# Gated attention and two mixtures on one Trainium2 core: the attention's products ordered by the shape of their tiles, and the chunk ends of two head pairs limited and inverted together

## The chip, the cores and the metric

The kernel runs on one core of a Trainium2 chip. Five engines work side by side, each through its own queue and in its own order: TensorE (PE; its weight loads are listed apart as PEld), VectorE (DVE), ScalarE (ACT), GpSimd (POOL) and SyncE (SP), which here issues most of the transfers. Semaphores hold an instruction back until what it needs is there. The metric is the device time of one execution in microseconds (us); lower is better.

## What is computed

```python
f = 1/(1+exp(-f_logit))                       # B,H,S,D = 4,8,768,48
for t in range(S):
    state = f[:,:,t,:,None]*state + einsum('bhd,bhe->bhde', k[:,:,t], v[:,:,t])
    y[:,:,t] = einsum('bhd,bhde->bhe', q[:,:,t], state)
x = y.transpose(0,2,1,3).reshape(B*S, H*D)    # 3072 tokens of 384
logits = x @ w_gate                           # 8 experts, 384 tokens each,
# given out greedily by descending logit; a token has one expert e
out[mask] = relu(x[mask] @ w1[e]) @ w2[e]     # 384 -> 1024 -> 384
h = out @ w_in;  result = (h*clip(h+3,0,6)/6) @ w_out      # 384 -> 2048 -> 384
```

All arrays are float32.

## The kernel before

The first fifth of the time is the attention (function `attention`); the routing of the tokens and the eight experts follow, and nothing of them is changed.

The attention goes over chunks of 128 time steps (C=128): 4 batches of 768 steps are 24 chunks (NCH), three of them a unit (U=384, NU=8). Two heads of 48 rows, padded to 64, share the 128 partitions, so that eight heads are four pairs (NP=4, index p). Within a chunk the recurrence is turned into products: `P` is the running product of the gates from the start of a chunk, `S` that from the other end divided by the whole product at the chunk's end, `QT` is q times P, `KH` is k times S, and the state is carried from chunk to chunk.

For each unit and pair, `tgroup` (L70 to L106) transposes f, k or q by three TensorE products (L83) into one of three PSUM buffers `pT`, and hands back a list of VectorE work: for f, after ScalarE has written the gate to `ff` (L87), the scan P (L91), the limit of its three chunk ends (L92), their reciprocal into the start values `m1` (L93) and the scan S (L94); for k the product KH (L96); for q the product QT (L103). `group` (L108) puts this work on VectorE's queue one or two calls later, and `ORD` (L198) gives the order of the twelve (pair, name) of a unit. A loop over j (L227) takes one chunk per step, and in it four groups of the next unit:

- `a_mm` (L134): the scores of chunk j+1, eight products from 64 rows to 128 columns, in two halves;
- `l_mm` (L189): the output of chunk j-1 for the store and the router's logits, four products of 128 by 128;
- `tg(0)`, `tg(1)`, `tg(2)`, `tg(3)`: the transposes, 128 by 128;
- `a_ev`: ScalarE copies the scores to SBUF (L139), GpSimd masks them (L140);
- `y_mm`: the output of chunk j, for each pair two products of the state (L161, 64 rows to 64 columns) and two of the masked scores (L163, 128 rows to 64 columns), summed in PSUM tile `pY`, which ScalarE copies (L165);
- `kv_mm` (L175): the chunk's part of the new state, 128 rows to 64 columns, added by VectorE (L182) and scaled by GpSimd (L183);
- `kt_mm` (L147): KH of chunk j+1 transposed, 128 by 128, copied by ScalarE (L148). Tile `pM` serves `kt_mm` and `l_mm` in turn.

Every sixth step starts a batch and has no state product; the step before it has no `kv_mm`, and the one before that no `kt_mm`. In the trace a product of float32 appears as two instructions on TensorE, a transpose as one. `prep` spreads the splitting of the last layer's weights over these steps: four VectorE operations per 128x512 tile (L876, L878, L880, L883), two of ScalarE and one of GpSimd (L664). `refill` reorders the next unit's f (ScalarE), k and q (GpSimd) and starts the loads after it.

Of the kernel before, what the change touches and what calls it, by code (L numbers as in the profile page):

```python
# [13 lines left out]
B,H,S,D=4,8,768,48  # L14
C=128; U=384; NP=4; NU=B*S//U; NCH=B*S//C
PMIN=2.0**-60; PB=3; MB=1

def attention(tc, q,k,v,f,wg, x_dram, lg, ident, pmin, ranges, prep, setup, spin):
    nc=tc.nc
    ctx=ExitStack()  # L20
    with ctx:
# [13 lines left out]
        M1=[]  # L35
        for i in range(2):
            t=cs.tile([128,U],F32,name=f"m1{i}"); nc.vector.memset(t,0.0); M1.append(t)
# [31 lines left out]
        KH={};QT={};PC={};tmp={}  # L69
        def tgroup(u,p,nm):  # L70
            if p==0 and nm=='f':
                t=wk.tile([128,NP,3],F32,name="pc",bufs=3); PC[u]=t
            if p==0 and nm=='k':
                KH[u]=KHB[u%2]
            if p==0 and nm=='q':
                t=wk.tile([128,NP,U],F32,name="qt"); QT[u]=t
            if u==0:
                n=ORD.index((p,nm))%4
                pt=ps.tile([128,C*3],F32,name=("pT","pA0","pT","pA1")[n],bufs=PB if n%2==0 else 1).rearrange("p (c r) -> p c r",r=3)
            else: pt=ps.tile([128,C,3],F32,name="pT",bufs=PB)  # L80
            x=perm[nm]
            for r in range(3):
                nc.tensor.transpose(pt[:,:,r],x[:,r,p].rearrange("p a d -> p (a d)"),ident)  # L83
            pf=pt.rearrange("p c r -> p (c r)")
            if nm=='f':
                ff=FF[p%2]
                nc.scalar.activation(ff[:,:U],pf,AF.Identity,bias=half[:,0:1],scale=0.5)  # L87
                P=wk.tile([128,U],F32,name="P",bufs=3); S_=wk.tile([128,U],F32,name="S")
                tmp[u,p]=(P,S_)
                V=nc.vector; m1=M1[p%2]; ends=lambda t: t.rearrange("p (c t) -> p c t",t=C)[:,:,C-1]  # L90
                return ([lambda: V.tensor_tensor_scan(P,m0,ff[:,:U],1.0,op0=OP.max,op1=OP.mult),  # L91
                         lambda: V.tensor_scalar(PC[u][:,p],ends(P),PMIN,None,op0=OP.max)],  # L92
                        [lambda: V.reciprocal(ends(m1),PC[u][:,p]),  # L93
                         lambda: V.tensor_tensor_scan(S_[:,::-1],ff[:,1:U+1][:,::-1],m1[:,::-1],1.0,op0=OP.mult,op1=OP.max)])  # L94
            elif nm=='k':
                return [lambda: nc.vector.tensor_mul(KH[u][:,p],pf,tmp[u,p][1])],[]  # L96
            else:
                if u==0:
                    t=wk.tile([128,2,NP,C],F32,name="am").rearrange("p s a c -> p (s a c)")[:,:U]
                    nc.scalar.copy(t,pf)  # L100
                    nc.gpsimd.tensor_tensor(out=QT[u][:,p],in0=t,in1=tmp[u,p][0],op=OP.mult)
                def whole_q():
                    if u>0: nc.vector.tensor_mul(QT[u][:,p],pf,tmp[u,p][0])  # L103
                    if p==NP-1:
                        nc.vector.tensor_tensor(out=pmin,in0=pmin,in1=PC[u].rearrange("p a b -> p (a b)"),op=OP.min)
                return [whole_q],[]  # L106
        prev=([],[]); rest=[]; late=[]
        def group(new,fill=None,flush=False):  # L108

# [12 lines left out]
                for op in prev[0]: op()  # L122
                prev=([],prev[1])
        AM={};KT={};pA={}
        def a_mm(j,hf):
            u,c=divmod(j,3)
            if hf==0:
                pA[j]=[]
                for s in range(2):
                    t=ps.tile([128,NP,C],F32,name=f"pA{s}"); pA[j].append(t)  # L130
            for p in (0,1) if hf==0 else (2,3):
# [9 lines left out]
        def kt_mm(j):  # L141
# [8 lines left out]
        YT={}  # L150
        def y_mm(j):
            u,c=divmod(j,3); first=j%6==0
            vr=raw['v',u]; cc=slice(c*C,(c+1)*C)
            last=j==NCH-1
            yt=wk.tile([128,NP,C],F32,name="yt")
            if not last: py=ps.tile([128,NP,C],F32,name="pY")
            for p in range(NP):
                if last and p%2==0: py=ps.tile([128,NP,C],F32,name=f"pA{p//2}")
                rows=[slice(64*s,64*s+64) for s in range(2)]
                if not first:  # L160
                    for r in rows: nc.tensor.matmul(py[r,p],St[j%2][r,p],QT[u][r,p,cc],start=True,stop=False)  # L161
                for s,r in enumerate(rows):
                    nc.tensor.matmul(py[r,p],vr[:,c,2*p+s],AM[j][:,s,p],start=first,stop=True)  # L163
# [148 lines left out]
class Routing:  # L312
# [714 lines left out]
```

## Time and profile before

| | us |
|---|---|
| median of 3 runs | 912.87 (912.25 to 913.35) |
| the profiled execution, its own time | 914.29 |
| its span in the profile | 912.3 |
| TensorE busy | 865.5 (95%) |
| VectorE busy | 542.2 (59%) |
| ScalarE, GpSimd busy | 370.5, 300.8 |
| attention's loop, from the first scores to the last logits | 17.78 to 199.74 |

A matmul's busy time overlaps that of its neighbours, so the distance between starts tells more than the busy share. "issue" is idle time for which the profile shows no awaited event.

### The profile page before, as it was taken

To read this page: it belongs to the slowest core of one execution; us is meant where nothing else is said; L and a number is where in the kernel's file an instruction comes from. 1 tells how busy PE (TensorE), PEld (TensorE's weight loads), DVE (VectorE), ACT (ScalarE), POOL (GpSimd) and SP (SyncE) were. 2 spreads that over 40 slices of the span, in tenths; PEclk is the share of its full clock that TensorE was granted. 3 is DMA by queue.
4 is the path that set the end of the run, shared out by engine and by line. 5 is a ranking of instruction groups with operands and counts; after the bars stand their busy time and mean duration, and the time that the engine had idled before them with its cause. 6 is when DMAs were issued, how large, how long until landed. Compare 5 with 4: busy or idle time off the path is not lost.

```text
span 912.3 us, 16113 instructions
## 1 busy us (share of the span) xinstructions
PE 865.5 (95%) x6086; PEld 787.8 (86%) x6086; DVE 542.2 (59%) x1410; ACT 370.5 (41%) x741; POOL 300.8 (33%) x378
## 2 busy tenths in 40 slices
PE   7999999997897869999999999999999999999995
PEld 6767777776787769989999999999999999999995
DVE  7889888735867893584476465565575422431331
ACT  4555555422344351443144235415432642542331
POOL 7666654313311551242042214312340341331001
PEclk9999999995898999999999999999999999999998
DMA  9674694125122430221121112121220221110000
GB/s 248 184 190 98 176 256 102 35 70 166 36 70 75 143 95 18 78 79 35 35 79 53 61 38 68 42 73 44 61 87 4 75 83 32 53 52 27 1 1 31
DMA packets 77159, 71.92 MB, mean 79 GB/s; under 512 B 29200, under 2 KB 65040, under 8 KB 77072
## 3 DMA queue, kind: packets, MB, share of 16 engines
q1 hardware_dynamic: 74000, 61.37, 23.7%
q0 software_dynamic: 3072, 9.44, 3.2%
q8 instruction: 49, 0.80, 0.4%
q14 instruction: 38, 0.31, 0.1%
HBM read 61.35 MB, written 9.44 MB: 78 GB/s over the span
## 4 chain that ended last, share of the span: by engine, by line
PE 56%; issue 14%; DVE 9%; ACT 3%; POOL 2%; DMA 1%; SPq 0%; POOLq 0%; ACTq 0%; DVEq 0%
PE pF L667 8%; PE acc L667 8%; PE pF L668 8%; PE pF L669 8%; PE acc L669 7%; PE acc L668 7%; DVE ga L800 2%; PE pY L163 1%; PE pY L161 1%; PE pM L189 1%; POOL wol L664 1%; ACT ga L799 1%; PE pA L134 1%; PE pT L83 1%; DVE q_Lm L418 1%
## 5 line engine op out<-in xcount | busy, mean ns | idle before, releaser
L667 PE MATMUL pF<-xh,wih 128*128 128x384 f32 x384 | 134.1, 349 | 0.6 <-ACT xh L784 0.6
L667 PE MATMUL acc<-woh,hh 128*128 128x384 f32 x384 | 133.8, 348 | 0.0
L800 DVE SCALAR_TENSOR_TENSOR ga<-ga,pF 128x384 f32<-128x384 f32 x128 | 70.8, 553 | 101.8 <-ACT ga L799 101.5
L669 PE MATMUL acc<-wol,hh 128*128 128x384 f32 x384 | 131.2, 342 | 0.0
L668 PE MATMUL acc<-woh,hl 128*128 128x384 f32 x384 | 131.0, 341 | 0.0
L669 PE MATMUL pF<-xl,wih 128*128 128x384 f32 x384 | 130.5, 340 | 0.0
L668 PE MATMUL pF<-xh,wil 128*128 128x384 f32 x384 | 130.4, 340 | 0.0
L664 POOL TENSOR_TENSOR w1l<-wst,w1h 128x512 fp32r<-128x512 f32 x42 | 55.1, 1312 | 193.0 <-ACT w1h L663 193.0
L799 ACT ACTIVATE ga<-pF,three 128x384 f32<-128x384 f32 x128 | 74.1, 579 | 97.0 <-PE pF L669 96.9
L802 ACT CAST hh<-ga 128x384 fp32r<-128x384 f32 x128 | 65.7, 513 | 105.2 <-DVE ga L800 105.2
L803 DVE TENSOR_TENSOR hl<-ga,hh 128x384 fp32r<-128x384 f32 x128 | 71.4, 558 | 59.9 <-ACT hh L802 59.5
L664 POOL TENSOR_TENSOR w2l<-wst,w2h 128x384 fp32r<-128x384 f32 x58 | 60.1, 1040 | 112.2 <-ACT w2h L663 108.3
L765 ACT ACTIVATE hh<-pF 128x384 fp32r<-128x384 f32 x64 | 31.5, 492 | 127.0 <-PE pF L669 121.1
L766 DVE SCALAR_TENSOR_TENSOR hl<-pF,hh 128x384 fp32r<-128x384 f32 x64 | 35.6, 556 | 77.8 <-ACT hh L765 77.3
L667 PEld LDWEIGHTS pF<-xh,wih 128*128 128x128 f32 x384 | 73.0, 190 | 1.9 <-ACT xh L784 0.9
L669 PEld LDWEIGHTS acc<-wol,hh 128*128 128x128 f32 x384 | 73.5, 191 | 0.0
L668 PEld LDWEIGHTS acc<-woh,hl 128*128 128x128 f32 x384 | 73.5, 191 | 0.0
L667 PEld LDWEIGHTS acc<-woh,hh 128*128 128x128 f32 x384 | 73.4, 191 | 0.1
L669 PEld LDWEIGHTS pF<-xl,wih 128*128 128x128 f32 x384 | 72.9, 190 | 0.3 <-DVE xl L785 0.3
L668 PEld LDWEIGHTS pF<-xh,wil 128*128 128x128 f32 x384 | 73.0, 190 | 0.0
L667 PE MATMUL pF<-xh,w1h 128*128 128x384 f32 x192 | 67.3, 350 | 0.6 <-ACT xh L735 0.6
L669 PE MATMUL acc<-hl,w2h 128*128 128x384 f32 x192 | 65.1, 339 | 2.2 <-DVE hl L766 2.2
(289 smaller groups left out, 1799.0 us busy)
## 6 DMA issues: line engine op xcount, KB each, us to landing
wst<-in_moe_w_dram SPq DMA_DIRECT2D x58, 192.0 KB, 2.4
wst<-in_moe_w_dram SPq DMA_DIRECT2D x42, 256.0 KB, 2.7
pw<-in_moe_w_in_dram SPq DMA_DIRECT2D x12, 512.0 KB, 4.0
pw<-in_moe_w_out_dram SPq DMA_DIRECT2D x16, 384.0 KB, 3.1
v<-in_v_dram SPq DMA_DIRECT2D x24, 192.0 KB, 5.1
x_dram<-y SPq DMA_DIRECT2D x24, 192.0 KB, 3.8
fr<-in_f_logit_dram SPq DMA_DIRECT2D x7, 576.0 KB, 5.4
kr<-in_k_dram SPq DMA_DIRECT2D x7, 576.0 KB, 5.1
```

Of the source, the lines that this page charges most:

```text
L83: nc.tensor.transpose(pt[:,:,r],x[:,r,p].rearrange("p a d -> p (a d)"),ident)
L134: nc.tensor.matmul(pA[j][s][:,p],KH[u][r,p,c*C:(c+1)*C],QT[u][r,p,c*C:(c+1)*C],start=True,stop=True)
L664: eng_lo.tensor_tensor(out=lo, in0=raw, in1=hi.bitcast(F32), op=OP.subtract)
L667: nc.tensor.matmul(out, ahi, bhi, start=start, stop=False)
L668: nc.tensor.matmul(out, alo, bhi, start=False, stop=False)
L669: nc.tensor.matmul(out, ahi, blo, start=False, stop=stop)
L765: nc.scalar.activation(hh,p,AF.Relu)
L766: s.defer(2,lambda: nc.vector.scalar_tensor_tensor(hl,p,0.0,hh.bitcast(F32),op0=OP.max,op1=OP.subtract))
L799: nc.scalar.activation(a,p,AF.Relu,bias=s.three[:,0:1])
L800: late(f,1,lambda: nc.vector.scalar_tensor_tensor(g,a,6.0,p,op0=OP.min,op1=OP.mult))
L802: late(f,1,lambda: nc.scalar.copy(gh,g))
L803: late(f,3,lambda: nc.vector.tensor_tensor(out=gl,in0=g,in1=gh.bitcast(F32),op=OP.subtract))
```

## The change

1. **Order of the products.** The two halves of `a_mm` become one. `tg(0)`, `l_mm` and `tg(1)` now come first; then `y_mm` part 0 does all state products of chunk j, then `a_mm` of chunk j+1, then `y_mm` part 1 all score products of chunk j, then `kv_mm`, `tg(2)`, `kt_mm`, `tg(3)`. One PSUM tile holds the sums of all four pairs between the two parts of `y_mm`.
2. **Chunk ends in pairs.** P of two pairs stands in one tile; the limit and the reciprocal are one operation each on six values per partition, after the second scan. `ORD` brings the two f of such a pair one after the other, and the second S is done one call after the first.
3. The places of `prep`'s pieces are moved (`PREP`: two, one and three calls in the three steps of a unit, where it was two in each), and `refill` of f, q and k follows the new order.

```diff
-                P=wk.tile([128,U],F32,name="P",bufs=3); S_=wk.tile([128,U],F32,name="S")
...
-                return ([lambda: V.tensor_tensor_scan(P,m0,ff[:,:U],1.0,op0=OP.max,op1=OP.mult),
-                         lambda: V.tensor_scalar(PC[u][:,p],ends(P),PMIN,None,op0=OP.max)],
-                        [lambda: V.reciprocal(ends(m1),PC[u][:,p]),
-                         lambda: V.tensor_tensor_scan(S_[:,::-1],ff[:,1:U+1][:,::-1],m1[:,::-1],1.0,op0=OP.mult,op1=OP.max)])
+                if p%2==0: PP[u,p//2]=wk.tile([128,2,U],F32,name="P")
+                P2=PP[u,p//2]; P=P2[:,p%2]; pp=slice(p-1,p+1)
...
+                ops=[lambda: V.tensor_tensor_scan(P,m0,ff[:,:U],1.0,op0=OP.max,op1=OP.mult)]
+                if p%2==0: return ops,[]
+                return (ops+[lambda: V.tensor_scalar(PC[u][:,pp],ends(P2),PMIN,None,op0=OP.max)],
+                        [lambda: V.reciprocal(ends(m1),PC[u][:,pp]),SF[u,p-1]])
...
+                return [whole_q],([] if p%2 else [SF[u,p+1]])
...
+            if part==0:
...
+                for p in range(NP):
+                    for r in rows: nc.tensor.matmul(PY[j][p//2][r,p],St[j%2][r,p],QT[u][r,p,cc],start=p==0 or last and p==2,stop=False)
+                return
...
-        ORD=[(0,'f'),(1,'f'),(0,'k'),(0,'q'),(2,'f'),(1,'k'),(1,'q'),(3,'f'),(2,'k'),(2,'q'),(3,'k'),(3,'q')]
+        ORD=[(0,'f'),(1,'f'),(0,'q'),(0,'k'),(2,'f'),(3,'f'),(1,'q'),(1,'k'),(2,'q'),(2,'k'),(3,'q'),(3,'k')]
...
-            if j+1<NCH: a_mm(j+1,0)
+            tg(0)
             if 0<=j-1<NCH: l_mm(j-1)
-            if j+1<NCH: a_mm(j+1,1)
-            tg(0)
+            tg(1)
             while later: later.pop(0)()
             if ti==2: refill(tu+1,'f')
+            if 0<=j<NCH: y_mm(j,0)
             if j+1<NCH:
+                a_mm(j+1)
                 a_ev(j+1,0)
                 a_ev(j+1,1)
-            if 0<=j<NCH:
-                y_mm(j)
-            tg(1)
+            if 0<=j<NCH: y_mm(j,1)
             if j>=0: kv_mm(j)
             tg(2)
             if j+1<NCH: kt_mm(j+1)
+            if ti==2: refill(tu+1,'q')
+            tg(3)
             if ti==2: refill(tu+1,'k')
-            tg(3)
-            if ti==2: refill(tu+1,'q')
```

TensorE's queue in a full step before, from the logits of one chunk on (the second half of the scores, the transposes, the output, the state, KH's transposes):

```order
L189 MATMUL pM<-sw,yt 128x104 x4
L134 MATMUL pA_558<-qt,kh_115 128x128
...
L83 MATMUL pT<-ident,pmf 128x128 x3
L161 MATMUL pY<-qt,St_116 64x128 x2
L163 MATMUL pY<-am,v_110 64x128 x2
...
L175 MATMUL pK<-v_110,kt 64x48 x8
L83 MATMUL pT<-ident,pmk 128x128 x3
L147 MATMUL pM<-ident,kh_115 128x128 x4
L83 MATMUL pT<-ident,pmq 128x128 x3
L134 MATMUL pA_672<-qt,kh_115 128x128
```

State and score products alternate four times, two and two, and the next scores follow the last transposes. The same step after the change:

```order
L195 MATMUL pM<-sw,yt 128x104 x4
L81 MATMUL pT<-ident,pmf 128x128 x3
L163 MATMUL pY<-qt,St_114 64x128 x8
L135 MATMUL pA_582<-qt,kh_113 128x128
...
L169 MATMUL pY<-am,v_108 64x128 x8
L181 MATMUL pK<-v_108,kt 64x48 x8
L81 MATMUL pT<-ident,pmq 128x128 x3
L148 MATMUL pM<-ident,kh_113 128x128 x4
L81 MATMUL pT<-ident,pmk 128x128 x3
L81 MATMUL pT<-ident,pmf 128x128 x3
```

The products of a kind now stand together, and between KH's transposes (L148) and the next logits (L195) there are six transposes where there were three and half of the scores.

VectorE's queue before, where two pairs' gates are worked on (P and S are the scans, pc the limited ends, m_ the reciprocals, pm the weight pieces):

```order
L92 TENSOR_SCALAR pc<-P 128x3
L93 RECIPROCAL m_102<-pc 128x3
L880 SCALAR_TENSOR_TENSOR pm<-pw,pm 128x512
L91 SCALAR_TENSOR_TENSOR P<-m_99,ff_122 128x384
L94 SCALAR_TENSOR_TENSOR S<-ff_120,m_102 128x384
L92 TENSOR_SCALAR pc<-P 128x3
L182 TENSOR_TENSOR St_116<-St_116,pK 128x4x48
L93 RECIPROCAL m_104<-pc 128x3
L96 TENSOR_TENSOR kh_114<-pT,S 128x384
L94 SCALAR_TENSOR_TENSOR S<-ff_122,m_104 128x384
```

The state's addition (L182) had the first pair's scan S ahead of it. After the change, at the same kind of place:

```order
L93 SCALAR_TENSOR_TENSOR P<-m_99,ff_120 128x384
L95 TENSOR_SCALAR pc<-P 128x6
L188 TENSOR_TENSOR St_116<-St_116,pK 128x4x48
L96 RECIPROCAL m_102<-pc 128x6
L105 TENSOR_TENSOR qt<-pT,P 128x384
L91 SCALAR_TENSOR_TENSOR S<-ff_118,m_102 128x384
```

One limit and one reciprocal serve both pairs, and both S scans now stand behind the state's addition.

## Rows read from the trace of the kernel before

**Rows 1.** The page: VectorE's busy tenths in 40 slices, and the chain that ended last.

```profile
DVE  7889888735867893584476465565575422431331
...
PE 56%; issue 14%; DVE 9%; ACT 3%; POOL 2%; DMA 1%; SPq 0%; POOLq 0%; ACTq 0%; DVEq 0%
```

**Rows 2.** Busy time by stretch: one step, the attention's parts, just behind it.

```profile
core 0: us, PE busy (x) PEld busy (x) DVE busy (x) ACT busy (x) POOL busy (x), PEclk, DMA share, GB/s
...
74.92:83.02 8.10, 8.10 (x90) 5.83 (x89) 8.10 (x15) 5.10 (x11) 3.43 (x3) 1.00 0.50 93
...
28.75:99.72 70.97, 70.03 (x759) 50.83 (x757) 64.02 (x122) 40.48 (x80) 43.77 (x65) 1.00 0.63 164
99.72:175.35 75.63, 75.07 (x811) 54.89 (x809) 63.99 (x133) 39.83 (x79) 39.20 (x69) 1.00 0.51 135
175.35:199.74 24.39, 24.31 (x284) 17.50 (x282) 6.42 (x33) 9.21 (x18) 5.44 (x11) 1.00 0.10 34
199.74:224.96 25.22, 20.09 (x255) 17.45 (x253) 13.56 (x50) 5.28 (x11) 5.99 (x5) 0.63 0.52 170
```

**Rows 3.** TensorE's instructions in one full step: start, busy us, line, tiles, count.

```profile
36.85 1.14 PE L189 MATMUL pM<-sw,yt 128*128 128x104 f32 x8
37.92 0.71 PE L134 MATMUL pA<-qt,kh 64*128 64x128 f32 x8
38.57 0.55 PE L83 MATMUL pT<-ident,pmf 128*128 128x128 f32 x3
39.05 0.44 PE L161 MATMUL pY<-qt,St 64*64 64x128 f32 x4
39.41 0.44 PE L163 MATMUL pY<-am,v 128*64 128x128 f32 x4
...
41.99 0.55 PE L83 MATMUL pT<-ident,pmf 128*128 128x128 f32 x3
...
43.45 0.60 PE L147 MATMUL pM<-ident,kh 128*128 128x128 f32 x4
43.89 0.49 PE L83 MATMUL pT<-ident,pmq 128*128 128x128 f32 x3
```

**Rows 4.** The weight loads ahead of one such group, with the idle time before them.

```profile
39.41 0.20 PEld L163 LDWEIGHTS pY<-am,v 128*64 128x64 f32 x4 [0.17 <-issue]
```

**Rows 5.** TensorE in a step that starts a batch: score products without state products.

```profile
162.68 1.09 PE L163 MATMUL pY<-am,v 128*64 128x128 f32 x16
163.70 0.55 PE L83 MATMUL pT<-ident,pmk 128*128 128x128 f32 x3
```

**Rows 6.** VectorE's groups from 28.75 to 175.35 us: busy us, mean ns.

```profile
L91 DVE TENSOR_TENSOR_SCAN P<-m,ff 128x384 f32<-128x384 f32 x25 | 28.0, 1121 | 7.2 <-ACT ff L87 6.8
L94 DVE TENSOR_TENSOR_SCAN S<-ff,m 128x384 f32<-128x384 f32 x26 | 26.2, 1008 | 0.0
L92 DVE TENSOR_SCALAR pc<-P 128x3 f32<-128x3 f32 x25 | 11.7, 466 | 0.4
L93 DVE RECIPROCAL m<-pc 128x3 f32<-128x3 f32 x25 | 4.4, 176 | 0.5
```

**Rows 7.** All scans P: shortest, median and longest in ns.

```profile
L91 DVE TENSOR_TENSOR_SCAN P<-m,ff x32: 941/992/1701, 6.2 to 169.5; 128x384 f32<-128x384 f32 x32
```

**Rows 8.** The copy of KH's transposes, and the logits that wait for it.

```profile
44.09 0.58 ACT L148 COPY kt<-pM 128x512 f32<-128x512 f32 x1 [0.86 <-PE pM L147]
...
68.09 0.59 ACT L148 COPY kt<-pM 128x512 f32<-128x512 f32 x1
...
68.74 1.14 PE L189 MATMUL pM<-sw,yt 128*128 128x104 f32 x8 [0.60 <-ACT kt L148]
```

**Rows 9.** TensorE in the last steps, which have no transposes of a next unit.

```profile
180.45 0.65 PE L147 MATMUL pM<-ident,kh 128*128 128x128 f32 x4
...
181.84 1.14 PE L189 MATMUL pM<-sw,yt 128*128 128x104 f32 x8
...
188.33 1.14 PE L189 MATMUL pM<-sw,yt 128*128 128x104 f32 x8
```

More of the change, by code (lines that the diff above doesn't have):

```diff
@@ L34, in attention @@
         nc.vector.memset(m0.rearrange("p (c t) -> p c t",t=C)[:,:,0:1],1.0)
-        M1=[]
-        for i in range(2):
-            t=cs.tile([128,U],F32,name=f"m1{i}"); nc.vector.memset(t,0.0); M1.append(t)
+        m1=cs.tile([128,2,U],F32,name="m1"); nc.vector.memset(m1,0.0)
         SW=cs.tile([128,NP,2*D+8],F32,name="sw"); nc.vector.memset(SW,0.0)
@@ L68, in reorder @@
             else: nc.gpsimd.tensor_scalar(o,x,1.0,0.0,op0=OP.mult,op1=OP.add)
-        KH={};QT={};PC={};tmp={}
+        KH={};QT={};PC={};PP={};SS={};SF={}
         def tgroup(u,p,nm):
@@ L87, in tgroup, with suffix @@
                 nc.scalar.activation(ff[:,:U],pf,AF.Identity,bias=half[:,0:1],scale=0.5)
[L88 to L94 removed]
+                if p%2==0: PP[u,p//2]=wk.tile([128,2,U],F32,name="P")
+                P2=PP[u,p//2]; P=P2[:,p%2]; pp=slice(p-1,p+1)
+                V=nc.vector; ends=lambda t: t.rearrange("p a (c t) -> p a c t",t=C)[:,:,:,C-1]
+                def suffix():
+                    SS[u,p]=wk.tile([128,U],F32,name="S",bufs=3)
+                    V.tensor_tensor_scan(SS[u,p][:,::-1],ff[:,1:U+1][:,::-1],m1[:,p%2,::-1],1.0,op0=OP.mult,op1=OP.max)
+                SF[u,p]=suffix
+                ops=[lambda: V.tensor_tensor_scan(P,m0,ff[:,:U],1.0,op0=OP.max,op1=OP.mult)]
+                if p%2==0: return ops,[]
+                return (ops+[lambda: V.tensor_scalar(PC[u][:,pp],ends(P2),PMIN,None,op0=OP.max)],
+                        [lambda: V.reciprocal(ends(m1),PC[u][:,pp]),SF[u,p-1]])
             elif nm=='k':
[L96 removed]
+                return [lambda: nc.vector.tensor_mul(KH[u][:,p],pf,SS[u,p])],[]
             else:
@@ L100, in tgroup @@
                     nc.scalar.copy(t,pf)
-                    nc.gpsimd.tensor_tensor(out=QT[u][:,p],in0=t,in1=tmp[u,p][0],op=OP.mult)
+                    nc.gpsimd.tensor_tensor(out=QT[u][:,p],in0=t,in1=PP[u,p//2][:,p%2],op=OP.mult)
                 def whole_q():
-                    if u>0: nc.vector.tensor_mul(QT[u][:,p],pf,tmp[u,p][0])
+                    if u>0: nc.vector.tensor_mul(QT[u][:,p],pf,PP[u,p//2][:,p%2])
                     if p==NP-1:
                         nc.vector.tensor_tensor(out=pmin,in0=pmin,in1=PC[u].rearrange("p a b -> p (a b)"),op=OP.min)
-                return [whole_q],[]
+                return [whole_q],([] if p%2 else [SF[u,p+1]])
         prev=([],[]); rest=[]; late=[]
@@ L124, in attention, with a_mm @@
         AM={};KT={};pA={}
-        def a_mm(j,hf):
+        def a_mm(j):
             u,c=divmod(j,3)
[L127 to L131, printed above, removed]
+            pA[j]=[]
+            for s in range(2):
+                t=ps.tile([128,NP,C],F32,name=f"pA{s}"); pA[j].append(t)
+            for p in range(NP):
                 for s in range(2):
@@ L149, in kt_mm, with y_mm @@
             KT[j]=kt
-        YT={}
-        def y_mm(j):
+        YT={};PY={}
+        def y_mm(j,part):
             u,c=divmod(j,3); first=j%6==0
@@ L154, in y_mm @@
             last=j==NCH-1
+            rows=[slice(64*s,64*s+64) for s in range(2)]
+            if part==0:
+                if last: PY[j]=[ps.tile([128,NP,C],F32,name=f"pA{i}") for i in range(2)]
+                else: PY[j]=[ps.tile([128,NP,C],F32,name="pY")]*2
+                if first: return
+                for p in range(NP):
+                    for r in rows: nc.tensor.matmul(PY[j][p//2][r,p],St[j%2][r,p],QT[u][r,p,cc],start=p==0 or last and p==2,stop=False)
+                return
             yt=wk.tile([128,NP,C],F32,name="yt")
-            if not last: py=ps.tile([128,NP,C],F32,name="pY")
             for p in range(NP):
[L158 to L161, printed above, removed]
+                py=PY[j][p//2]
                 for s,r in enumerate(rows):
-                    nc.tensor.matmul(py[r,p],vr[:,c,2*p+s],AM[j][:,s,p],start=first,stop=True)
+                    nc.tensor.matmul(py[r,p],vr[:,c,2*p+s],AM[j][:,s,p],start=first,stop=first or p==NP-1 or last and p==1)
                 if last and p%2: nc.scalar.copy(yt[:,p-1:p+1],py[:,p-1:p+1])
@@ L226, in attention @@
         constants,early=setup()
+        PREP=((0,2),(0,),(0,1,2))
         for j in range(-1,NCH+1):
@@ L232, in tg @@
             def tg(i):
-                group(tgroup(*g[i]) if g[i] is not None else ([],[]),(lambda: next(prep,None)) if j>=0 and i%2==0 else None,(ti,i)==(2,3))
-            if j+1<NCH: a_mm(j+1,0)
+                group(tgroup(*g[i]) if g[i] is not None else ([],[]),(lambda: next(prep,None)) if j>=0 and i in PREP[ti] else None,(ti,i)==(2,3))
             if j==NCH: spin(lambda: ps.tile([128,384],F32,name="pT",bufs=PB),TAIL[0])
+            tg(0)
             if 0<=j-1<NCH: l_mm(j-1)
             if j==NCH: spin(lambda: ps.tile([128,384],F32,name="pT",bufs=PB),TAIL[1])
-            if j+1<NCH: a_mm(j+1,1)
-            tg(0)
+            tg(1)
             while later: later.pop(0)()
             if ti==2: refill(tu+1,'f')
+            if 0<=j<NCH: y_mm(j,0)
             if j+1<NCH:
+                a_mm(j+1)
                 a_ev(j+1,0)
                 a_ev(j+1,1)
-            if 0<=j<NCH:
-                y_mm(j)
-            tg(1)
+            if 0<=j<NCH: y_mm(j,1)
             if j>=0: kv_mm(j)
```

## The prediction, made before the changed kernel was run

> **What bounds the kernel now.** I read first the page's slices and its chain: VectorE is at 7 to 9 tenths in the first eight of 40 slices, the attention, and nowhere that high for long later, and the chain of the whole run is TensorE's with 14% "issue" [rows 1]. Next the busy time by stretch: from 28.75 to 175.35 us, nineteen steps with transposes of a next unit, TensorE shows 70.03+75.07=145.1 us of 146.6, but VectorE 64.02+63.99=128.0, or 87% [rows 2]. So TensorE's queue sets the pace and VectorE stands close behind. Then TensorE's instructions in one full step, which takes 8.1 us: they leave no gap between groups, yet a group of four state or score products takes (41.99-39.05)/8=0.3675 us from its start to the next [rows 3], while sixteen score products in a row take 163.70-162.68=1.02 us [rows 5]. Twelve more instructions cost 0.6525, 0.0544 each. So 0.3675-4x0.0544=0.15 us of each group of four isn't product but pause, and the weight loads show it as 0.17 us idle, "issue", each time that the tile's shape changes [rows 4]. The transposes behind KH's, of the same 128 by 128 shape, follow at 0.44 us for four, 0.11 each, without it [rows 3]. The pause goes with the change of shape.
>
> **The change part by part.**
>
> *The order on TensorE.* A full step before has fifteen changes of shape: into the first half of the scores, into the logits, into the second half, into the transposes, eight into and within the output, out of it, into the state's products and out of them. After it there are four: transposes to state products, to scores, to score products (and on to the state's, the same 128 by 64), to transposes. Eleven go. A batch's last step, without `kv_mm`, loses nine, its first, without state products, five. Of the nineteen steps thirteen are full or lack only KH's transposes, three are last, three first: 13x11+3x9+3x5=185 pauses, at 0.15 us 27.7 us. TensorE's own need in this stretch falls from 145.1 to 117.4 us.
>
> *A new wait on TensorE.* KH's transposes and the logits share one tile, so the logits wait until ScalarE has copied KH's. From the start of those transposes to the copy's start it is 44.09-43.45=0.64 us, the copy takes 0.58, and the logits start 68.74-68.09-0.59=0.06 behind it [rows 3, 8]: 1.28 us. Before, the transposes of group 3 and half of the scores lay between, now two groups of transposes: 0.44+6x0.11=1.10 us. I expect 0.18 us of waiting in sixteen steps, 2.9 us; where ScalarE hands the copy over late, more, as the 0.60 us before the logits at 68.74 show [rows 8]. TensorE: 117.4+2.9=120.3 us.
>
> *The pairing on VectorE.* Limit and reciprocal take 466 and 176 ns in the mean [rows 6], the pair's operations on six values instead of three about the same. Half of 25 go: 12.5x0.642=8.0 us. VectorE's need falls from 128.0 to 120.0 us. TensorE bounded that stretch, so this alone would hide; with the pauses gone it is needed.
>
> *What else moves.* VectorE's state addition waits for `kv_mm` and now stands in front of the reciprocal and both S scans, and behind those wait KH and, through the two gate buffers, ScalarE's next gates. In a step that puts the queue 0.5 to 1 us behind; against it the scores of a new unit, which need the last KH, come after two groups of transposes, the logits and the state products instead of first, some 2.6 us later (0.33 for each group of transposes, 0.92 for the logits without their pause, 1.02 for sixteen state products). The two shifts are of the same size, so I put them into the overlap loss below. The weight pieces keep their number. Refills and loads keep theirs too: the order of q's and k's follows that of their last use, and f's refill still has more than half a step ahead of the next gates. DMA was busy for 0.63 and 0.51 of these stretches [rows 2]; packed into 125 us instead of 146.6 that is 0.67 in the mean, which still leaves room. Cost taken as nothing; if that cover fails, it costs a wait for reordered inputs at a unit's border.
>
> *The sum of the stretch.* Two queues that each need 120 us and wait for one another can't both run without a gap. At no loss the stretch would take 120.3 us, 26.3 less. VectorE's share was 64.02/70.97=90% where it was not the bound [rows 2]; at 90% it needs 120.0/0.90=133.3 us, 13.3 less. I take 96%, nearer to the upper end, because three buffers of transposed input let TensorE run ahead of VectorE: 120.2/0.96=125.2 us, 21.4 less.
>
> *The tail.* The steps without a next unit take 188.33-181.84=6.49 us [rows 9]. Eight changes of shape go, 1.2 us. But now nothing stands between KH's transposes and the logits; the distance of 181.84-180.45=1.39 us between them stays, and half of the scores (38.57-37.92=0.65 us [rows 3]), which lay in it, comes on top elsewhere. Net 0.5 us in three steps, and in the last output seven pauses, 1.05 us: 2.5 us, bounds 1 and 4. VectorE is nearly idle there, 6.42 of 24.39 us.
>
> *The start.* Ahead of 28.75 us a few pauses go (two steps, at most ten pauses, 1.5 us), and the first S waits for the second P: 0.5 us, bounds 0 and 1.5.
>
> *Behind the attention* everything starts earlier by the same amount. In the 25 us there the granted clock is 0.63 in the mean [rows 2]: about three quarters of that time at 1.2 GHz, the rest at 2.4. Where the edges fall against the new start is not settled by this trace; at 4 us of such work more or less at the lower level, my estimate is 2 us either way.
>
> Sum: 21.4+2.5+0.5=24.4 us off the profiled execution's 914.3 gives 889.9. The median of the runs was 1.4 us below that execution, so 888.5.
>
> **The rivals.**
>
> *VectorE takes over harder.* The in-order waits (state addition before the scans, gates behind them) leave it 6 to 12% idle: stretch 128 to 136 us, 894 to 901. For it: both queues need the same time, so that every late hand-over costs. Against it: VectorE ran whole steps without a gap before, as from 74.92 to 83.02 us [rows 2].
>
> *TensorE's floor.* VectorE gets faster than its mean, since its short operations often waited (limit 466 ns in the mean), and 120.3 us or a little less is reached: 879 to 884.
>
> *The two row tiles no longer run side by side.* The state products of a pair's two heads go to one PSUM bank. Before, four took as long as four score products [rows 3], so they ran in twos. The Trainium skill (TensorEngine Tiling (Array Packing), Gotcha 1: PSUM Pressure) says that different row tiles cannot access the same PSUM bank simultaneously; by that rule the eight of them would go one after the other, against what this row shows for groups of two. If the long run of sixteen instructions did so, each would cost 0.0544 us more: 16x0.0544=0.87 us in some nineteen steps, 16.5 us of the gain, 905.
>
> *The pauses stay.* If the pause belonged to the turn between products that add into one tile and not to the shape, TensorE would keep its 145 us, and VectorE's saving would hide: 912. The transposes without pause and the sixteen score products speak against it.
>
> *Slower.* VectorE's scans stretch. They take 0.94 us at best and 1.70 at worst [rows 7]; the means were 1.12 and 1.01 [rows 6]. With the same GpSimd and DMA work in less time, each could be longer. VectorE needs 120.0 us; at 51 scans it becomes the bound of the old time when a scan grows by (146.6-120.0)/51=0.52 us, to about 1.6. At 1.70 for all, 32.6 us more, the stretch takes 152.6 us, and with the tail's gain the whole 916.
>
> **How the numbers follow.** Forecast, 884 to 894: 0.55. VectorE harder, 894 to 901: 0.22. The floor, 879 to 884: 0.12. Row tiles in turn, near 905: 0.04. Pauses stay, 912: 0.03. Slower, 916: 0.04. The predicted time is the first one's, 888.5. The range of 881 to 899 holds the forecast, most of the harder case and half of the floor, about 0.8. About 0.2% is what a measurement of this kernel can tell from no change, so faster has 0.93, same 0.03, slower 0.04.
>
> **What would show it right or wrong.** In the changed profile a full step should take 6.5 to 6.9 us instead of 8.1; idle "issue" before weight loads should be left at four places in a step; sixteen state products should take about 1.0 us; VectorE should be busy 95% or more of the stretch up to its end near 154 us; and the logits should show a wait of some 0.2 us for the copy of KH's transposes. If steps are short but unit borders show TensorE waiting for KH or for the gates, the first rival is right. If VectorE's scans average over 1.3 us, the last one is near. If sixteen state products take 1.9 us, it is the row tiles. The forecast would be wrong altogether if the pauses are seen again between equal shapes.

## The result and the profile after

The changed kernel takes 900.59 us in the median of four runs (897.71 to 903.43), the kernel before 913.11 beside it (912.25 to 913.4): a ratio of 0.9866, 95% interval 0.9848 to 0.9885. So it is faster by 12.5 us where 24.4 were forecast, and 900.59 lies above the range of 881 to 899. The profiled execution is the slowest of the four, 903.43 us, with a span of 901.7; what follows explains that one. The page's slices and chain, which answer to [rows 1]:

```profile
DVE  7989699556867973673575465565574422431331
...
PEclk9999899977998999999999999999999999999998
...
PE 54%; issue 14%; DVE 10%; ACT 3%; POOL 2%; DMA 1%; SPq 0%; POOLq 0%; ACTq 0%; DVEq 0%
```

VectorE is no fuller than before in the attention's slices, though the attention is shorter. Busy time by stretch, with the columns of [rows 2]: the nineteen steps, their first nine and next ten, the tail, the 25 us behind it, and then three single steps.

```profile
core 0: us, PE busy (x) PEld busy (x) DVE busy (x) ACT busy (x) POOL busy (x), PEclk, DMA share, GB/s
28.32:166.60 138.28, 126.10 (x1561) 109.50 (x1562) 125.33 (x227) 80.88 (x157) 91.21 (x137) 0.96 0.62 159
28.32:98.92 70.60, 63.38 (x757) 54.81 (x757) 63.65 (x109) 39.88 (x78) 48.19 (x72) 0.93 0.66 170
98.92:166.60 67.68, 62.73 (x805) 54.70 (x806) 61.68 (x119) 41.00 (x80) 43.02 (x66) 1.00 0.57 147
166.60:188.82 22.22, 20.87 (x290) 18.32 (x290) 6.66 (x32) 9.11 (x18) 6.36 (x13) 1.00 0.11 38
188.82:214.33 25.51, 20.20 (x255) 17.56 (x253) 13.54 (x50) 5.28 (x11) 5.58 (x5) 0.64 0.54 171
134.04:140.68 6.64, 6.62 (x88) 5.87 (x89) 6.43 (x10) 4.71 (x9) 3.62 (x5) 1.00 1.06 213
42.43:52.23 9.80, 8.24 (x88) 7.15 (x88) 7.51 (x12) 4.72 (x9) 7.25 (x11) 0.83 0.77 193
86.77:98.92 12.15, 9.51 (x89) 8.43 (x89) 8.49 (x13) 3.83 (x8) 6.41 (x11) 0.72 0.83 236
```

Against [rows 2] the first nine steps are shorter by 70.97-70.60=0.4 us, the next ten by 75.63-67.68=8.0, the tail by 24.39-22.22=2.2. An undisturbed full step takes 6.64 us where it took 8.10. So the pauses are gone, and something else fills most of the first half. TensorE's instructions in that undisturbed step, which answer to [rows 3]:

```profile
134.04 1.14 PE L195 MATMUL pM<-sw,yt 128*128 128x104 f32 x8
...
135.43 1.09 PE L163 MATMUL pY<-qt,St 64*64 64x128 f32 x16
136.45 1.16 PE L135 MATMUL pA<-qt,kh 64*128 64x128 f32 x16
137.54 1.09 PE L169 MATMUL pY<-am,v 128*64 128x128 f32 x16
138.47 0.62 PE L181 MATMUL pK<-v,kt 128*64 128x48 f32 x16
...
140.68 1.14 PE L195 MATMUL pM<-sw,yt 128*128 128x104 f32 x8
```

Sixteen state products take 136.45-135.43=1.02 us, just as sixteen score products did before [rows 5]. The two slow steps look different. In the first and the second of them (idle time before a group, and who ended it, in brackets):

```profile
45.43 1.72 PE L163 MATMUL pY<-qt,St 64*64 64x128 f32 x16 [1.54 <-POOL St L189]
47.09 2.08 PE L135 MATMUL pA<-qt,kh 64*128 64x128 f32 x16
49.09 1.10 PE L169 MATMUL pY<-am,v 128*64 128x128 f32 x16
...
90.85 1.97 PE L163 MATMUL pY<-qt,St 64*64 64x128 f32 x16 [2.62 <-POOL St L189]
92.75 2.08 PE L135 MATMUL pA<-qt,kh 64*128 64x128 f32 x16
94.76 1.97 PE L169 MATMUL pY<-am,v 128*64 128x128 f32 x16
```

TensorE waits for the scaled state (`St`, L189; before, L183), and the groups behind the wait take nearly twice their 1.02 to 1.09 us: they ran at the lower level of the clock, 1.2 GHz: the granted clock is 0.50 from 47.09 to 49.09 us, and 0.83 and 0.72 in the mean of these two steps. GpSimd's queue ahead of the first wait, with VectorE's addition to the state (L188), on which the scaling waits:

```profile
36.73 2.90 POOL L66 TENSOR_SCALAR pmq<-qr 128x384 f32<-128x384 f32 x3
39.60 1.90 POOL L66 TENSOR_SCALAR pmk<-kr 128x384 f32<-128x384 f32 x3
40.59 0.35 DVE L188 TENSOR_TENSOR St<-St,pK 128x192 f32<-128x192 f32 x1
42.39 2.35 POOL L141 TENSOR_SCALAR_AFFINE_SELECT am<-am 128x512 f32<-128x512 f32 x2
44.70 0.67 POOL L189 TENSOR_TENSOR St<-St,pc 128x192 f32<-128x192 f32 x1
```

The sum was there at 40.94, when GpSimd was at the last of six reorderings of k and q; a small constant for the routing (0.92 us) and the two masks (2.35 us) still stood ahead of the scaling, which came at 44.70. Ahead of the second wait there is a weight piece's low half among them too. The larger waits of TensorE's products in the nineteen steps, in us, times, longest, and below them the wait of its weight loads (PEld) for the copy of KH's transposes:

```profile
PE pY L163 <- POOL St L189: 4.2, 2, 2.6
PE pM L195 <- ACT kt L149: 3.0, 5, 1.3
PE pM L148 <- DVE lg L197: 2.8, 3, 1.1
...
PEld pM L195 <- ACT kt L149: 7.7, 17, 1.6
```

The logits waited for that copy at nearly every step: the weight loads, which run ahead of the products, show 17 waits where the products' idle time shows five. From the start of KH's transposes to the logits it is 1.10 us without a wait (0.77 in the last of the nineteen steps, with one group of transposes between them); the sixteen distances come to 7.2 us more, leaving out 0.93 us of another wait. Ahead of the longest of these waits, ScalarE's queue had three reorderings of the next unit's f and three other copies before KH's, whose transposes started at 124.77:

```profile
124.00 1.36 ACT L65 ACTIVATE pmf<-fr 128x384 f32<-128x384 f32 x3
...
126.67 0.62 ACT L149 COPY kt<-pM 128x512 f32<-128x512 f32 x1
127.34 1.14 PE L195 MATMUL pM<-sw,yt 128*128 128x104 f32 x8 [1.31 <-ACT kt L149]
```

Last, VectorE's groups, which answer to [rows 6]; L882 is the first operation on a weight piece:

```profile
L91 DVE TENSOR_TENSOR_SCAN S<-ff,m 128x384 f32<-128x384 f32 x26 | 28.7, 1106 | 0.0
L93 DVE TENSOR_TENSOR_SCAN P<-m,ff 128x384 f32<-128x384 f32 x24 | 28.1, 1170 | 2.3 <-ACT ff L85 2.3
L98 DVE TENSOR_TENSOR kh<-pT,S 128x384 f32<-128x384 f32 x26 | 14.1, 543 | 0.1
L882 DVE TENSOR_SCALAR pm<-pm 128x512 f32<-128x512 f32 x12 | 10.5, 876 | 0.0
L95 DVE TENSOR_SCALAR pc<-P 128x6 f32<-128x6 f32 x12 | 4.8, 397 | 0.2
L96 DVE RECIPROCAL m<-pc 128x6 f32<-128x6 f32 x12 | 2.2, 184 | 0.1
```

Limit and reciprocal fell from 16.1 us [rows 6] to 7.0, yet VectorE's busy time fell by 2.7 only: S grew from 1008 to 1106 ns, P from 1121 to 1170.

### The profile page after: what moved, and what is told of

Read it like the earlier page. It is cut to its first block, busy times and chain, and to the rows that moved or that the text cites. A ratio compares the mean times of both kernels' runs of the same rounds, so it can differ in the third digit from the quotient of the medians.

```text
span 901.7 us, 16093 instructions
## 1 busy us (share of the span) xinstructions
PE 841.3 (93%) x6086; PEld 791.5 (88%) x6086; DVE 539.1 (60%) x1377; ACT 371.8 (41%) x741; POOL 308.3 (34%) x378
## 4 chain that ended last, share of the span: by engine, by line
PE 54%; issue 14%; DVE 10%; ACT 3%; POOL 2%; DMA 1%; SPq 0%; POOLq 0%; ACTq 0%; DVEq 0%
PE pF L673 8%; PE acc L673 8%; PE pF L674 8%; PE pF L675 8%; PE acc L675 8%; PE acc L674 7%; DVE ga L806 2%; POOL wol L670 1%; ACT ga L805 1%; DVE q_Lm L424 1%; PE pM L195 1%; DVE hl L809 1%; PE pA L135 1%; PE acc L383 1%; PE pY L169 1%
## 5 line engine op out<-in xcount | busy, mean ns | idle before, releaser
L673 PE MATMUL acc<-woh,hh 128*128 128x384 f32 x384 | 133.8, 348 | 0.0
L809 DVE TENSOR_TENSOR hl<-ga,hh 128x384 fp32r<-128x384 f32 x128 | 71.3, 557 | 59.9 <-ACT hh L808 59.6
```

Source lines behind the costliest of these rows:

```text
L673: nc.tensor.matmul(out, ahi, bhi, start=start, stop=False)
L809: late(f,3,lambda: nc.vector.tensor_tensor(out=gl,in0=g,in1=gh.bitcast(F32),op=OP.subtract))
```

## The experiments

Three causes were to be told apart for the 13 us that the stretch lacks: GpSimd's queue ahead of the state's scaling, TensorE's clock behind those waits, and VectorE as the bound. All edits are against the changed kernel unless said otherwise. Medians and ratios to the kernel before in the same comparison; the stretch, the busy times in it and the granted clock are from each profile:

| run | median us | ratio (95%) | stretch | VectorE | GpSimd | clock |
|---|---|---|---|---|---|---|
| the change | 900.59 | 0.987 (0.985 to 0.989) | 138.3 | 125.3 | 91.2 | 0.96 |
| order_only | 902.98 | 0.989 (0.985 to 0.992) | 138.3 | 126.9 | 89.5 | 0.95 |
| pairs_only | 916.53 | 1.004 (1.002 to 1.006) | 150.4 | 115.8 | 83.4 | 0.99 |
| state_first | 900.69 | 0.987 (0.985 to 0.990) | 136.8 | 126.8 | 88.8 | 0.98 |
| state_dve | 896.98 | 0.985 (0.981 to 0.988) | 134.0 | 128.9 | 82.5 | 0.99 |
| state_act | 901.96 | 0.988 (0.986 to 0.990) | 137.2 | 123.9 | 79.0 | 0.98 |
| fill | 897.39 | 0.982 (0.980 to 0.984) | 133.8 | 126.3 | 91.1 | 1.00 |
| free_pm | 896.00 | 0.982 (0.980 to 0.983) | 134.3 | 128.9 | 81.0 | 0.99 |
| free_unpaired | 905.77 | 0.992 (0.991 to 0.994) | 140.3 | 132.8 | 81.3 | 0.98 |
| less_dve | 888.24 | 0.972 (0.969 to 0.975) | 128.4 | 103.4 | 84.9 | 1.00 |
| less_pool | 894.09 | 0.980 (0.978 to 0.982) | 127.2 | 117.6 | 71.3 | 1.00 |
| prep_even | 894.86 | 0.982 (0.980 to 0.984) | 132.4 | 115.5 | 85.7 | 1.00 |
| best2 | 895.00 | 0.980 (0.976 to 0.983) | 129.7 | 120.6 | 74.9 | 1.00 |

### The two halves of the change

`order_only` keeps the new order of the products and has the chunk ends, `ORD`, `PREP` and refills of before; `pairs_only` keeps the new chunk ends, `ORD` and order of refills and has the order of the products of before, and `PREP`'s places too. So the third part of the change, `PREP`, stands in neither.

```diff
 order_only
-        ORD=[(0,'f'),(1,'f'),(0,'q'),(0,'k'),(2,'f'),(3,'f'),(1,'q'),(1,'k'),(2,'q'),(2,'k'),(3,'q'),(3,'k')]
+        ORD=[(0,'f'),(1,'f'),(0,'k'),(0,'q'),(2,'f'),(1,'k'),(1,'q'),(3,'f'),(2,'k'),(2,'q'),(3,'k'),(3,'q')]
-                if p%2==0: PP[u,p//2]=wk.tile([128,2,U],F32,name="P")
+                P=wk.tile([128,U],F32,name="P",bufs=3); S_=wk.tile([128,U],F32,name="S")
...
 pairs_only
-            if 0<=j<NCH: y_mm(j,0)
+            if 0<=j<NCH: y_mm(j)
```

> The changed order of TensorE's products, but each pair's chunk ends limited and inverted by itself, with the old order of the twelve transposes. Theory A (the changed kernel lost its gain where the state's scaling waits in GpSimd's queue behind masks and refills, and to the TensorE clock that falls after such a wait): the same queue stands there, TensorE's pauses go all the same, so 899 to 906, within 4 us of the changed kernel. Theory B (VectorE is the bound): without the pairing VectorE needs 8 us more in the attention, so about 908, 8 us above the changed kernel.

> The paired chunk ends and their order of transposes, with TensorE's old order of products. Both theories: TensorE keeps its fifteen changes of shape in a step and bounds the attention, VectorE's 8 us hide: 910 to 914. If it is faster by more than 3 us, VectorE already held TensorE up before.

Their stretches, order_only first:

```profile
29.76:168.05 138.29, 126.58 (x1561) 110.66 (x1561) 126.86 (x248) 80.95 (x158) 89.51 (x134) 0.95 0.61 158
```

```profile
29.40:179.80 150.40, 146.68 (x1564) 106.74 (x1564) 115.80 (x231) 80.87 (x157) 83.36 (x134) 0.99 0.55 144
```

The order alone gives the whole gain of the stretch (146.6 to 138.3 us); its median and that of the full change aren't told apart. The pairing alone is 3.5 us slower than the kernel before, and above the 910 to 914 expected. It does save VectorE work, 128.0 to 115.8 us, even more than the 8.0 forecast, but TensorE's 146.7 us then stand ahead of it. Where the 3.5 us come from was not tested: in this trace P waits longer for its gates (26.2 us in all, 7.2 before), and the clock is lower from 66 to 80 us (0.89 and 0.86), behind a wait of 1.75 us. The same pairing that is worth 12.2 us of VectorE's time at the old pace is worth 126.9-125.3=1.6 at the new one.

### The state's scaling

`state_first` puts the masks behind the scaling in GpSimd's queue, `state_dve` and `state_act` move the scaling off GpSimd.

```diff
 state_first
+            masks.append(lambda: nc.gpsimd.affine_select(out=am, ...
             tg(2)
+            while masks: masks.pop(0)()
...
 state_dve
-                    nc.gpsimd.tensor_tensor(out=sn,in0=so,in1=pcb,op=OP.mult)
+                    nc.vector.tensor_tensor(out=sn,in0=so,in1=pcb,op=OP.mult)
...
 state_act
-                    nc.gpsimd.tensor_tensor(out=sn,in0=so,in1=pcb,op=OP.mult)
+                    for p in range(NP): nc.scalar.activation(sn[:,p],so[:,p],AF.Identity,scale=PC[u][:,p,c:c+1])
```

> The changed kernel, with the masks of the next scores put behind the state's scaling in GpSimd's queue; no work is added or left out. Theory A: the waits of 1.5 and 2.6 us for the state's scaling and the low clock behind them go, 8 us less than the profiled run of the changed kernel: 889 to 895. Theory B: VectorE's queue is as long as before, so as the changed kernel, 898 to 903.

> The changed kernel, with the state's scaling done by VectorE right behind its addition instead of by GpSimd. Theory A: the wait for GpSimd's queue goes as well, at the price of 0.3 us of VectorE in each step: 891 to 897. Theory B: VectorE's queue is 6 us longer, so slower than the changed kernel: 903 to 908.

> The changed kernel with the state's scaling on ScalarE (four operations of 48 columns per chunk) instead of GpSimd; VectorE's work is that of the changed kernel. If the attention is bound by VectorE (its operations at 125 us in the stretch of nineteen steps) and the wait for GpSimd's queue came on top: as state_dve less its 5 us of VectorE work, 892 to 895. If ScalarE's own queue makes the waits (the copy of KH's transposes): 898 or more.

In state_first the waits only move on. TensorE's waits in its stretch:

```profile
PE pM L148 <- DVE lg L197: 3.3, 3, 1.7
PE pY L163 <- POOL St L189: 1.2, 1, 1.2
...
PE pT L81 <- POOL pmk L66: 0.9, 1, 0.9
```

The wait for the state is 3.0 us shorter, the stretch 1.5, the median the same. In state_dve no wait for the state is left, and the stretch falls by 4.3 us; but VectorE is now busy for 128.9 of 134.0 us, 96%, which leaves it little room. In state_act the same wait goes to ScalarE's copy of KH's transposes, which stands behind the new work there:

```profile
PE pM L195 <- ACT kt L149: 8.0, 11, 1.3
```

So the wait behind GpSimd's queue is real, and taking it away alone gives a third of the missing 13 us at most: other waits grow in its place.

### The clock

`fill` leaves every wait in place and gives TensorE 7 and 12 idle products of 128 by 128 ahead of the state products of the two slow steps.

```diff
                 if first: return
+                for _ in range({3:7,9:12}.get(j,0)): nc.tensor.matmul(PY[j][0][:,0],ident,ident,start=True,stop=True)
```

> The changed kernel, with 7 and 12 idle products of TensorE (0.22 us each) put where its profiled run waited 1.5 and 2.6 us for the state's scaling and its clock then fell: before the state products of chunks 3 and 9. They fill the wait and shorten nothing else. If the low clock behind those waits costs what the two steps show (1.6 and 2.9 us) and comes of the idle time: 3 to 5 us faster, 896 to 898, with granted clock 1.0 in both steps. If not: as the changed kernel or up to 2 us slower.

TensorE in the first of these steps, then the whole stretch:

```profile
44.22 1.73 PE L162 MATMUL pY<-ident 128*128 128x128 f32 x14
45.92 1.09 PE L164 MATMUL pY<-qt,St 64*64 64x128 f32 x16
```

```profile
28.83:162.61 133.78, 126.07 (x1600) 109.98 (x1600) 126.28 (x227) 80.61 (x157) 91.08 (x137) 1.00 0.66 163
```

The state products start as late as before, but take 1.09 us instead of 1.72, and the two steps fall from 9.80 and 12.15 us to 8.25 and 9.34. The stretch is 138.28-133.78=4.5 us shorter by added work, and the median of 897.39 lies in the expected 896 to 898: that is what the clock cost in the profiled execution of the change. The length of a wait alone doesn't say whether the clock falls. In less_dve, a run below, one of 1.89 us was followed by a granted clock of 1.00 (84.92 to 92.00 us):

```profile
84.92 1.09 PE L163 MATMUL pY<-qt,St 64*64 64x128 f32 x16 [1.89 <-POOL St L189]
```

### VectorE's need, and what lengthens it

`less_dve` leaves out three of four VectorE operations on each weight piece; `less_pool` leaves out GpSimd's low halves of these pieces and keeps VectorE's instructions; `prep_even` drops one line, so that the pieces come later and more evenly.

```diff
 less_dve
-                    V.tensor_scalar(m,m,2.0**-15,None,op0=OP.max)
-                    V.tensor_scalar(t,t,3,0x3ffffff8,op0=OP.logical_shift_left,op1=OP.bitwise_and)
-                    V.scalar_tensor_tensor(t,hw,0xC0000000,t,op0=OP.bitwise_and,op1=OP.bitwise_or)
...
 less_pool
-                split_raw(nc,r,hi,lo,nc.gpsimd)
+                if r.shape[-1]==512: nc.scalar.copy(hi,r)
+                else: split_raw(nc,r,hi,lo,nc.gpsimd)
...
+        nc.gpsimd.memset(wil.bitcast(F32),0.0)
...
 prep_even
-            if 0<=j<10: next(prep,None)
```

> The changed kernel without three of the four VectorE operations of each weight piece (36 operations, some 25 us of VectorE in the attention); the last layer's weights are then not what they should be. Nothing else is changed. Theory B: VectorE's load makes the waits, so they all shrink, to 884 to 890. Theory A: the wait for the state's scaling in GpSimd's queue stays, 893 to 899.

> The changed kernel without the GpSimd part of the weight pieces (12 operations of 1.4 us; the last layer's low weight halves are set to zero after the attention instead). VectorE's instructions are unchanged. If GpSimd's work stretches VectorE's operations, VectorE's busy time in the stretch falls from 125 us towards 120 and the time to 890 to 896. If only GpSimd's queue matters (the wait for the state), the time falls by up to 5 us but VectorE's operations keep their lengths.

> The changed kernel with the same weight pieces spread evenly over all 24 steps: ten VectorE operations, about 7 us, move from the first ten steps into the last four, where VectorE is nearly idle. If VectorE bounds: 5 to 7 us faster than the changed kernel, 893 to 896. If not: within 2 us of it, 899 to 902.

The stretch of less_pool and four of VectorE's groups in it:

```profile
28.36:155.53 127.17, 120.89 (x1561) 105.67 (x1561) 117.58 (x227) 80.75 (x157) 71.27 (x126) 1.00 0.65 171
```

```profile
L91 DVE TENSOR_TENSOR_SCAN S<-ff,m 128x384 f32<-128x384 f32 x26 | 26.7, 1029 | 0.0
L93 DVE TENSOR_TENSOR_SCAN P<-m,ff 128x384 f32<-128x384 f32 x24 | 26.0, 1085 | 2.3 <-ACT ff L85 2.3
L98 DVE TENSOR_TENSOR kh<-pT,S 128x384 f32<-128x384 f32 x27 | 14.7, 546 | 0.0
...
L882 DVE TENSOR_SCALAR pm<-pm 128x512 f32<-128x512 f32 x12 | 6.9, 577 | 0.0
```

This run shows that GpSimd's work lengthens VectorE's. VectorE executes the same 227 instructions; with 20 us less of GpSimd's work beside them they take 117.6 us instead of 125.3, S 1029 ns instead of 1106 and L882 577 instead of 876. The transfers are not what lengthened them: the DMA engines were busier here, 0.65 against 0.62. On TensorE's side the wait for the state shrinks to 0.4 us, that for VectorE's sum of the logits from 2.8 to 1.1, and the clock stays at full; the stretch is 138.28-127.17=11.1 us shorter. The weight loads' wait for KH's copy stays, 7.8 us. The profiled executions differ by less, 903.43-894.59=8.8 us: this kernel clears the tile of the low halves behind the attention, and from there to the first expert product it takes 29.2 us instead of 25.5.

In less_dve, with VectorE far from the bound, the median of 888.24 us lies in the range of theory B, though a part of the wait for the state stays, as theory A has it. TensorE's busy time is 120.3 of 128.4 us, and most of the rest are the waits for the state (2.4 us) and for KH's copy (4.0; 8.1 by the weight loads). GpSimd's instructions, left as they were, take 84.9 instead of 91.2 us: VectorE's work lengthens GpSimd's too. prep_even moves nine VectorE operations and some of GpSimd's out of the stretch; no lower clock is left in it, and 894.86 us lies in the expected 893 to 896:

```profile
28.49:160.91 132.42, 121.56 (x1561) 105.76 (x1561) 115.53 (x218) 77.83 (x153) 85.69 (x135) 1.00 0.60 161
```

### The pairing once the other waits are gone, and a better kernel

`gates4` is state_dve with four gate buffers; `free_pm` adds a copy of the logits by ScalarE; `free_unpaired` makes these three edits to order_only. `best1` is state_act, four gate buffers and prep_even, `best2` free_pm and prep_even, `best3` prep_even with the low halves on VectorE.

```diff
 gates4, free_pm, free_unpaired, best1, best2
-                ff=FF[p%2]
+                ff=FF[p]
...
 free_pm, free_unpaired, best2
+                nc.scalar.copy(lq,px[:,:,2*D:])
...
 best3
-                split_raw(nc,r,hi,lo,nc.gpsimd)
+                split_raw(nc,r,hi,lo,nc.vector if r.shape[-1]==512 else nc.gpsimd)
```

> As state_dve, with four gate buffers instead of two, so that ScalarE's next gates no longer wait for the scan S of two pairs before. Theory A (waits chain up in ScalarE's and GpSimd's in-order queues, VectorE itself has room): the 5.3 us of TensorE's waits for the copy of KH's transposes and the 1.3 us for a gate go, 4 to 6 us below state_dve: 891 to 893. Theory B (VectorE has no room): the wait goes on to VectorE's products, within 2 us of state_dve: 895 to 899.

> As gates4, and the logits are copied out of the shared tile by ScalarE (0.2 us a step) so that KH's transposes no longer wait for VectorE's sum. Theory A: another 2 to 3 us, 888 to 891, near the time forecast for the change. Theory B: as gates4 within 2 us.

> As free_pm, but with each pair's chunk ends by themselves and the old order of transposes. If the pairing saves VectorE 8 us and VectorE bounds: 5 to 8 us above free_pm. If its saving is only the operations' own 0.14 and 0.18 us (the rest of the 0.47 us having been a wait that falls to a neighbour) or VectorE doesn't bound: within 3 us of free_pm.

> state_act and prep_even together, with four gate buffers. If VectorE bounds and the waits in the other queues come on top: 885 to 890. If the effects don't add: 892 or more.

> prep_even with the state's scaling on VectorE, four gate buffers and the logits copied by ScalarE: all three waits removed where VectorE now has room (115.5 of 132.4 us). If the waits add to VectorE's need: 3 to 5 us below prep_even, 890 to 892. If VectorE is full again (120 us in the stretch): as prep_even, 894 to 896.

> prep_even with the low half of the weight pieces made by VectorE (0.56 us each) instead of GpSimd (1.4 us each), so that GpSimd neither stretches VectorE's operations nor holds up the state: VectorE gains what it loses, and the state's wait (1.8 us) and the refills' go: 890 to 893. If the new VectorE work comes on top undiminished: 896 or more.

gates4 took 899.06 us (ratio 0.985, 0.983 to 0.986): the gate buffers were not the bound. free_pm took 896.00, between its two expectations, in a stretch as long as that of gates4 (134.3 and 134.5 us). free_pm and free_unpaired differ by 905.77-896.00=9.8 us, compared on the same chip, where 5 to 8 or less than 3 were expected. VectorE is close to full in both (128.9 of 134.3 and 132.8 of 140.3 us), and without the pairing TensorE waits for KH, the last of VectorE's chain, 9.3 us in all where free_pm has 1.4:

```profile
PE pT L83 <- DVE kh L96: 9.3, 7, 1.9
```

Of the 8.4 us between the two profiled executions 6.0 lie in the stretch, where VectorE's own time differs by 3.8 only. So the pairing, with the `ORD`, `PREP` and refills that belong to it, is worth no less than the 8.0 us forecast once VectorE is close to full and TensorE's other waits are gone, but by waits more than by VectorE's time; in the kernel as changed it isn't seen. best1 took 897.15 us (0.983, 0.982 to 0.985) and best3 897.25 (0.983, 0.980 to 0.985): in neither did the gains add up to the 885 to 890 and 890 to 893 that were possible. prep_even at 894.86 and best2 at 895.00 are the fastest that compute everything and aren't told apart; in best2 VectorE is at 120.6 us again, as its second expectation has it. prep_even, one line less, beats both kernels: against the change 5.7 us in the medians (5.3 by their distances to the kernel before), in ranges that don't overlap (894.59 to 896.89, 897.71 to 903.43).

## Why the prediction was wrong

**What bounded the kernel, and the pauses: right.** The full step takes 6.64 us, between the 6.5 and 6.9 named, 1.46 less than before; eleven pauses less the new wait would be 1.47. "issue" idle time ahead of weight loads of the four kinds of products fell from 26.3 to 6.0 us, left at two places of a step and not at the four named: ahead of the state products and of the scores. Less the 0.17 us of waiting at its end the undisturbed step needs 6.47 us, where 8.10 less eleven pauses is 6.45, so the 117.4 us worked out for TensorE hold. Its busy time where the clock stays up, 120.3 to 121.6 us (less_dve, less_pool, prep_even), is longer because short waits of 0.2 us for KH's copy don't show as idle time of the products.

**The copy of KH's transposes: right in the undisturbed step, wrong in the sum.** The logits at the start and the end of the undisturbed step come 1.33 and 1.27 us after KH's transposes, 0.23 and 0.17 us late, where 0.18 was expected. Over the sixteen places it is 7.2 us where 2.9 were forecast.

**Tail, start, behind: right.** 2.2 us (2.5 forecast), 28.75-28.32=0.4 (0.5), and behind the attention 0.3 us lost (0, give or take 2), with 25.51 us at a clock of 0.64 where [rows 2] have 25.22 at 0.63.

**The sum of the stretch: wrong.** 8.3 us instead of 21.4. One cost taken as nothing and two terms of the sum failed.

The first is in "What else moves", with "Cost taken as nothing". It counted refills and weight pieces, but didn't walk GpSimd's queue, in which they stand ahead of the state's scaling. At 8.1 us a step that queue had slack; at 6.6 it hasn't in two of the first nine steps. Two waits of TensorE come of it, 4.2 us, and behind them the lower clock, 4.5 us more (fill).

The second is a term of the sum that was mis-sized, the wait for KH's copy: 7.2 us for 2.9. The prediction said that it would be more where ScalarE hands the copy over late, and put no price on that. Ahead of the longest of these waits stood f's refill: there the prediction looked at the time left before the next gates, and not at the copies behind it in ScalarE's queue. less_dve and less_pool keep the wait (8.1 and 7.8 us by the weight loads), so neither VectorE's load nor the low halves on GpSimd make it. In best3, where the pieces come at other times, it is 0.17 to 0.23 us in fourteen of the sixteen places (4.8 us by the weight loads).

The third is another mis-sized term: VectorE's need, 125.3 us instead of 120.0. The saving itself was underrated (9.1 us for 8.0), but the other operations grew. GpSimd's instructions, which lengthen them, filled 66% of the stretch where it was 57% before (91.2 of 138.3 and 83.0 of 146.6 us). That is the mechanism of the rival "Slower", at a small part of its price: P and S averaged 1.17 and 1.11 us, not 1.6. less_pool shows it with VectorE's instructions unchanged, 7.7 us. The Trainium skill (SBUF — State Buffer, section "Who interferes with whom") says that a VectorE instruction with two inputs in SBUF contends with GpSimd instructions that read SBUF, and that `tensor_scalar` can in a two-port mode. The trace agrees in the main: the scans, with two inputs, and L882, a `TENSOR_SCALAR`, are shorter in less_pool, and the product KH, which reads one of its inputs from PSUM, keeps its length (543 and 546 ns). It doesn't agree everywhere: L889, with two inputs in SBUF, took 709 ns in the change and 744 in less_pool.

On TensorE's queue the parts add up: 117.4 us of its own need, 7.2 for KH's copy, 4.2 for the state, 2.8 for VectorE's sum of the logits, 1.1 in two smaller waits and 4.5 for the clock make 137.2 of the 138.3 us. The forecast had 117.4, 2.9 and 4.9 of overlap loss, 125.2. So VectorE's longer operations reach TensorE directly only through the 2.8 us. They also lengthen GpSimd's (less_dve), and through them the wait for the state and the clock; how much of those is theirs isn't settled. What is shown is that taking away 20 us of GpSimd's work returns 11.1 of the missing 13.1 us. The share of 96% for the overlap was not far off: at less_pool VectorE is busy for 92% and TensorE for 95% of a stretch of 127.2 us, two above the forecast.

**The rivals.** "VectorE takes over harder" came nearest, 894 to 901, and 900.59 lies in it, which is luck in the main: its stretch of 128 to 136 us was 138.3. VectorE was idle for 9% of it, as the rival has it, but only 2.8 us of TensorE's waits are directly for VectorE's late work. state_first and state_dve show that the waits for the state came from GpSimd's queue, and fill that 4.5 us were the clock's. "The two row tiles" fell: sixteen state products take 1.02 us, where 1.9 was its sign. The rule of the Trainium skill (TensorEngine Tiling (Array Packing), Gotcha 1: PSUM Pressure) doesn't hold for these. "The pauses stay" fell with the 6.64 us. "The floor" wasn't reached.

## What to carry to other kernels

When the pauses of the engine that sets the pace are taken out, walk every other in-order queue at the new pace, GpSimd's among them: what stands ahead of the one instruction that the fast engine will wait for, and how dense is the side work there? A wait shifted to another full queue returns little; spreading the side work (one line) took the time down at least as far as the best move of the waiting instruction (894.86 and 896.98 us). A wait that is priced in an undisturbed step has to be priced again where the side work stands. And the busy time of VectorE isn't a constant to divide by: beside denser GpSimd work it grew.

## What the runs showed of the hardware

- A change of tile shape between state and score products (64x64 and 128x64, float32) held TensorE up for some 0.15 us [rows 3, 4]; without eleven of fifteen changes a step of 8.10 us took 6.64. Of the four left, two show idle time of 0.17 us ahead of the weight loads.
- Idle times of 1.54 and 2.62 us in an otherwise full stretch were followed by a granted clock of 0.83 and 0.72 in the step's mean; idle products in their place kept it at 1.00 and gave 4.5 us back. Another, of 1.89 us, left the clock at 1.00 (less_dve).
- State products of two row tiles into one PSUM bank ran as fast in a run of sixteen (1.02 us) as score products that use all rows.
- VectorE's 227 instructions took 125.3 us beside 91.2 us of GpSimd's work and 117.6 beside 71.3; the product KH, with one input from PSUM, took 543 and 546 ns. With less VectorE work GpSimd's took 84.9 us instead of 91.2.
